# Row 8 of the first batch's q by a transposed transfer, and two subtractions on other engines

## The chip, the cores and the metric

The kernel runs on one core of a Trainium2 chip. The metric is the device time of one execution in microseconds; the runs of the kernel before took 281.86 to 282.16 us, with a median of 281.95.

## What is computed

Linear attention with a softmax on q over its 64 columns and a softmax on k over its 576 rows, and then a two-layer network with a leaky ReLU between the layers:

```python
q_s = np.exp(q - np.max(q, axis=-1, keepdims=True))
q_s = q_s / (np.sum(q_s, axis=-1, keepdims=True) + 1e-09)
k_s = np.exp(k - np.max(k, axis=2, keepdims=True))
k_s = k_s / (np.sum(k_s, axis=2, keepdims=True) + 1e-09)
kv = np.einsum('bhsd,bhse->bhde', k_s, v)
attn = np.einsum('bhsd,bhde->bhse', q_s, kv)      # q, k, v: 8 batches, 8 heads, 576 rows, 64
x = attn.transpose(0, 2, 1, 3).reshape(4608, 512)
h = x @ w_in                                       # 512 x 2048
out = np.maximum(0.01 * h, h) @ w_out              # 2048 x 512
```

## The kernel before

The 4608 rows of `x` are worked through in nine tiles of 512 (t = 0 to 8), one batch of attention being 576 rows. A tile is 64 matmuls of `layer1` (L550) and 64 of `layer2` (L571), both on TensorE (PE in the profile), with the leaky ReLU on ScalarE (ACT, L559) between them. The attention of a later batch is done in between: its steps are hung up by hand with `at(t, u, ...)` and run after step u of tile t, so that the order on every engine is fixed by the text of the kernel. Each engine works through its own instructions in that order, and waits at an instruction whose inputs are not there.

A batch's q, k and v are loaded by SyncE (SP), which issues all loads, all transposed transfers and all stores one after the other; `raw` tiles hold them as 128 partitions x 4 head pairs x 9 rows x 64. A partition holds nine rows, so the transposed q has row blocks R = 0 to 8. `H0` and `H1` are the head pairs 0, 1 and 2, 3 of the tile; `R7` is rows 0 to 6, `RE` rows 7 and 8, `R3` row 8.

For k: `k_tree` (L153, VectorE, DVE) takes the maximum over nine rows in four steps, `k_allmax` the maximum over partitions, `k_sub` (L186) subtracts it, `k_exp` (L194, ScalarE) writes `ke`. For q: `q_max` (L229), `q_sub` (L291), `q_exp` (L299), `q_sum` (L308) and `q_norm` (L315). `v_cast` (L204 on ScalarE, L206 on GpSimd, POOL) makes bf16 of v. `kv` (L328) multiplies k by v on TensorE, `kd_make` (L348, L349) divides by k's sums, and `cross` (L464) multiplies the transposed q by it. q is transposed in one of two ways: on TensorE against the identity with a copy out of PSUM (`q_turn_first` L268 with `q_keep_first` L281 and L282; `q_transpose` L432 with `q_keep` L447), or by a DMA of SyncE (`q_turn` L538, `turn_next` L544).

Tile t = 1 needs row 8 of batch 0 and rows 0 to 6 of batch 1: `attend_next` (L525) computes them at step (0, 46), in tile 0's second layer, from batch 0's transposed row 8 in `qT` and from batch 1's `X1` (heads by transposed transfer) and `qT` (heads by TensorE). The steps of batch 1 that the change touches stand at (0, 20) to (0, 45). `more_loads` and `next_loads` are the two groups of loads that SyncE issues then. Batch 2 follows in `plan2`, its matmuls against transposed q in tile 1 (`qX` and the rest of `X1`, at step (1, 27)); the loads of batch 3 are issued at (1, 2). PSUM holds six 2 KB banks in `psB_pool` and two in `psO_pool`.

The hooks and loads around the change, as they stand before it:

```python
    def more_loads():
        ...
        load(v, 1, "v_raw", [(H0, ALLR), (H1, ALLR)], t)
        st[2]["k"] = load(k, 2, "k_raw", [(H0, ALLR)])

    def next_loads():
        turn_next(slice(0, 7 * 2 * D), slice(0, 7))
        load(q, 1, "q_raw", [(ALLH, RE)], st[1]["q"])
        load(k, 2, "k_raw", [(H1, ALLR)], st[2]["k"])
```

Of the kernel before, what the change touches and what calls it, by code (L numbers as in the profile page):

```python
# [9 lines left out]
BF16 = mybir.dt.bfloat16  # L10
# [10 lines left out]
R = 9  # L21
# [4 lines left out]
def kernel(  # L26
# [9 lines left out]
    nc = tc.nc  # L36
# [10 lines left out]
    P = 128  # L47
# [27 lines left out]
    def load(src, b, name, cuts, t=None):  # L75
        t = raw(name) if t is None else t
        flat = src[b].rearrange("h s d -> (h s d)").rearrange(
            "(hl p r d) -> p hl r d", hl=HL, p=P, r=R
        )
        for hs, rs in cuts:  # L80
            nc.sync.dma_start(
                out=t[:, hs, rs].rearrange("p h r d -> p h (r d)"),
                in_=flat[:, hs, rs].rearrange("p h r d -> p h (r d)"),
            )
        return t

    ALLH, ALLR = slice(0, HL), slice(0, R)
# [95 lines left out]
    def k_sub(eng, b, hs):  # L183
        ks = st[b]["k"][:, hs]
        n = hs.stop - hs.start
        eng.tensor_tensor(  # L186
            out=ks,
            in0=ks,
            in1=st[b]["kall"][:, hs].unsqueeze(2).to_broadcast([P, n, R, D]),
            op=ALU.subtract,  # L190
        )

    def k_exp(b, hs):
        nc.scalar.activation(  # L194
            out=st[b]["ke"][:, :, hs].rearrange("p r h d -> p h r d"),
            in_=st[b]["k"][:, hs],
            func=AF.Exp,
        )
# [27 lines left out]
    def q_max(b, rs, hs=ALLH):  # L226
        n, m = rs.stop - rs.start, hs.stop - hs.start
        st[b]["qmax", rs.start, hs.start] = o = small_pool.tile([P, HL, n], FP32, name="qmax")[:, 0:m]
        nc.vector.tensor_reduce(out=o, in_=st[b]["q"][:, hs, rs], axis=AX.X, op=ALU.max)  # L229
# [58 lines left out]
    def q_sub(eng, b, rs, hs=ALLH):  # L288
        n, m = rs.stop - rs.start, hs.stop - hs.start
        qs = st[b]["q"][:, hs, rs]  # L290
        eng.tensor_tensor(  # L291
            out=qs,
            in0=qs,
            in1=st[b]["qmax", rs.start, hs.start].unsqueeze(3).to_broadcast([P, m, n, D]),
            op=ALU.subtract,
        )
# [154 lines left out]
    def cross(b, gg, outs, rows):  # L451
        for hp in range(2):
            for hh in range(2):
                half = slice(hp * D, (hp + 1) * D)
                ls = slice(hh * L, (hh + 1) * L)
                if b == 1 and rows.start == R7.stop:
                    rhs = st[b]["X1"][:, R7.stop :].rearrange("c (r g) l -> c g r l", g=2)[:, gg, :, ls]
                elif b == 1 and gg == 0:
                    rhs = st[b]["X1"][:, rows, ls]
                elif "qX" in st[b]:  # L460
                    rhs = st[b]["qX"].rearrange("c (r g) (h l) -> c g h r l", g=2, h=2)[:, gg, hh, rows]
                else:
                    rhs = st[b]["qT"][:, 2 * hh + gg, rows]
                nc.tensor.matmul(  # L464
                    outs[hp][hh * D : (hh + 1) * D].rearrange("p (r l) -> p r l", l=L),
                    lhsT=kd0[half, gg, hh, hp] if b == 0 else kd2[b % 2][half, gg, hh],
                    rhs=rhs[half],
                    start=True,
                    stop=True,
                )  # L470
# [72 lines left out]
    def turn_next(cols, blocks):  # L543
        nc.sync.dma_start_transpose(  # L544
            out=st[1]["X1"][:, blocks], in_=st[1]["qe"].rearrange("p r h d -> p (r h d)")[:, cols]
        )
# [35 lines left out]
    def at(t, u, *fns):  # L582
        while t > 0 and u >= 32:
            t, u = t + 1, u - 32
        hooks.setdefault((t, u), []).extend(fns)
# [87 lines left out]
    def more_loads():  # L673
        st[1]["v"] = t = raw("v_raw")
        nc.scalar.copy(out=t[0:1, 0, 0, 0:1], in_=identf[0:1, 0:1])
        load(v, 1, "v_raw", [(H0, ALLR), (H1, ALLR)], t)
        st[2]["k"] = load(k, 2, "k_raw", [(H0, ALLR)])

    def next_loads():
        turn_next(slice(0, 7 * 2 * D), slice(0, 7))  # L680
        load(q, 1, "q_raw", [(ALLH, RE)], st[1]["q"])
        load(k, 2, "k_raw", [(H1, ALLR)], st[2]["k"])
        st[2]["q"] = load(q, 2, "q_raw", [(ALLH, ALLR)])
        st[2]["v"] = load(v, 2, "v_raw", [(ALLH, ALLR)])
# [1 line left out]

    at(0, 20, lambda: k_begin(1), lambda: q_begin(1), lambda: k_tree(1, H0), lambda: k_tree(1, H1))
    at(0, 20, lambda: q_max(1, R7, H0), lambda: q_sub(nc.gpsimd, 1, R7, H0), lambda: k_allmax(1))
    at(0, 20, lambda: k_sub(nc.vector, 1, H1), lambda: k_sub(nc.gpsimd, 1, slice(0, 1)))
    at(0, 20, lambda: k_sub(nc.vector, 1, slice(1, 2)))  # L690
    at(0, 20, lambda: q_max(1, R7, H1), lambda: q_sub(nc.gpsimd, 1, R7, H1))
    at(0, 27, more_loads)
    at(0, 31, lambda: q_exp(1, R7, H0), lambda: q_sum(1, R7, H0), lambda: q_norm(1, R7, H0))
    at(0, 31, lambda: k_exp(1, H1), lambda: k_exp(1, H0), lambda: v_cast(nc.scalar, 1, 0))
    at(0, 32, lambda: q_exp(1, R7, H1), lambda: q_sum(1, R7, H1), lambda: q_norm(1, R7, H1))
    at(0, 32, next_loads)
    at(0, 32, lambda: v_cast(nc.scalar, 1, 1))
    at(0, 44, lambda: kv(1), lambda: kd_make(1))
    at(0, 45, lambda: q_turn_first(1, 1, R7), lambda: q_keep_first((nc.scalar, nc.vector), 1, 1, R7))
    at(0, 45, lambda: q_transpose(0, 8, 1), lambda: q_keep(nc.scalar, 0, 8, 1))  # L700
    at(0, 45, lambda: k_begin(2), lambda: q_begin(2), lambda: k_tree(2, H0, slice(0, 1)))
    at(0, 46, attend_next)
    at(1, 0, lambda: q_max(1, RE), lambda: q_sub(nc.gpsimd, 1, RE))
    at(1, 5, lambda: q_exp(1, RE))
# [3 lines left out]

    def plan2():
        b = 2  # L710
        at(1, 0, lambda: k_tree(b, H0, slice(1, 4)), lambda: k_tree(b, H1))
        at(1, 3, lambda: q_max(b, XR[0]), lambda: q_sub(nc.gpsimd, b, XR[0]))
        at(1, 3, lambda: k_allmax(b), lambda: k_sub(nc.vector, b, H0), lambda: k_sub(nc.vector, b, H1))
        at(1, 6, lambda: q_max(b, XR[1]), lambda: q_sub(nc.gpsimd, b, XR[1]))
        at(1, 11, lambda: q_exp(b, XR[0]), lambda: q_sum(b, XR[0]), lambda: q_norm(b, XR[0]))
        at(1, 13, lambda: v_cast(nc.gpsimd, b, 0), lambda: v_cast(nc.gpsimd, b, 1))
        at(1, 14, lambda: q_sum(1, RE), lambda: q_norm(1, RE))
        at(1, 15, lambda: k_exp(b, ALLH), lambda: q_turn(b, XR[0]))
        at(1, 15, lambda: turn_next(slice(7 * HL * D, R * HL * D), slice(7, 11)))
        at(1, 16, lambda: q_exp(b, XR[1]), lambda: q_sum(b, XR[1]), lambda: q_norm(b, XR[1]))  # L720
        at(1, 17, lambda: q_turn(b, XR[1]))
        at(1, 17, lambda: load_all(4))
        at(1, 23, lambda: kv(b))
        at(1, 24, lambda: kd_make(b))
        at(1, 27, lambda: attend_all(b, (XR[0],)), lambda: attend_all(1, (RE,)))
# [180 lines left out]
```

## Time and profile before

| what | value |
|---|---|
| median of the runs | 281.95 us |
| the profiled execution | 281.87 us, its span 280.1 us |
| TensorE busy | 273.5 us |
| VectorE / ScalarE / GpSimd busy | 162.0 / 160.0 / 50.1 us |
| read from HBM / written | 36.70 / 9.44 MB |

The span runs from the first to the last instruction of the program; the 1.8 us between it and the execution's time lie around it. A row of the timeline has the start, the duration, the engine, the line, the operation, out<-in and the shape; `x2` means that two equal instructions that follow each other are shown as one row, and a bracket at the end gives the idle time ahead of it and what ended it. A row of the transfers has what is written and read, the queue, the kind, the count, the size and the median time from issue to landing. The stretch of the edit on ScalarE reads:

```profile
34.79 1.16 ACT L194 ACTIVATE ke<-k_raw 128x1152 bf16<-128x1152 f32 x1 [0.85 <-DVE k_raw L186]
36.72 1.16 ACT L194 ACTIVATE ke<-k_raw 128x1152 bf16<-128x1152 f32 x1 [0.77 <-DVE k_raw L186]
37.79 1.14 ACT L204 CAST vb<-v_raw 128x1152 bf16<-128x1152 f32 x1
39.43 0.95 ACT L299 ACTIVATE qe<-q_raw 128x896 bf16<-128x896 f32 x1 [0.51 <-POOL q_raw L291]
40.29 1.14 ACT L204 CAST vb<-v_raw 128x1152 bf16<-128x1152 f32 x1
44.38 0.53 ACT L281 COPY qT<-psum_q 128x448 bf16<-128x448 bf16 x1 [2.95 <-PE psum_q L268]
44.80 0.38 ACT L447 COPY qT<-psum_qt 128x256 bf16<-128x256 bf16 x1
```

Twice there ScalarE waits for a subtraction by VectorE (L186), and once for one by GpSimd (L291).

### The profile page before, as it was taken

The page shows a single profiled execution, that of the slowest core. Times are in us where ns is not written, and L with a number is a line of the kernel's source. Part 1 is how long each engine was busy: PE and PEld are TensorE (multiplying, and loading weights), DVE is VectorE, ACT ScalarE, POOL GpSimd, SP SyncE. Part 2 cuts the span into 40 slices and gives each one's busy share as a digit, 9 for nine tenths or more (in the row PEclk, how much of TensorE's full clock was granted, in tenths as well). Part 3 has the DMA queues.
Part 4 walks back from the last instruction along what each step waited for, and adds up shares of the span by engine and source line. Part 5 has one row for each costly group of instructions (what it writes and reads, how often), then busy time and mean ns, then how long its engine had stood idle before and what let it go on. Part 6 is the DMA issues. An engine that isn't in the chain of part 4 may idle for free.

```text
span 280.1 us, 4898 instructions
## 1 busy us (share of the span) xinstructions
PE 273.5 (98%) x1963; PEld 133.4 (48%) x1963; DVE 162.0 (58%) x229; ACT 160.0 (57%) x284; POOL 50.1 (18%) x54
## 2 busy tenths in 40 slices
PE   8799999999999999999999999999999999999994
PEld 3378645444444454445444444444444444444443
DVE  2986898999999959957794588543700000000021
ACT  4977574783498277754676448744844364146400
POOL 2947530257203004000500060000000000000000
PEclk9999999999999999999999999999999999999999
DMA  7999999899692498099309930333033300330033
GB/s 245 333 209 322 248 297 328 311 325 271 214 392 81 92 363 291 1 269 396 81 0 302 361 79 2 84 77 75 1 87 75 73 4 0 75 75 2 0 75 75
DMA packets 38678, 46.15 MB, mean 165 GB/s; under 512 B 17536, under 2 KB 21888, under 8 KB 38656
## 3 DMA queue, kind: packets, MB, share of 16 engines
q1 hardware_dynamic: 35136, 41.53, 47.1%
q0 software_dynamic: 3360, 4.20, 8.6%
q8 instruction: 15, 0.25, 0.3%
q10 hardware_dynamic: 160, 0.13, 0.1%
q14 instruction: 7, 0.06, 0.1%
HBM read 36.70 MB, written 9.44 MB: 165 GB/s over the span
## 4 chain that ended last, share of the span: by engine, by line
PE 94%; DVE 2%; DMA 2%; ACT 0%; issue 0%; SPq 0%
PE pout L571 45%; PE ph L550 45%; DMA k_raw<-in_k_dram 2%; PE po L464 2%; DVE t L153 1%; PE pokv L328 1%; PE pkv L328 1%; PE pkv L406 0%; DVE k_raw L397 0%; PE psum_qt L432 0%; PE psum_q L268 0%; ACT ke L194 0%; DVE kmax L153 0%; DVE kd L421 0%; PE pokv L464 0%
## 5 line engine op out<-in xcount | busy, mean ns | idle before, releaser
L571 PE MATMUL pout<-w_out_sb,gj 128*128 128x512 bf16 (+2 forms) x592 | 127.7, 373 | 0.0
L550 PE MATMUL ph<-xT,w_in_sb 128*128 128x512 bf16 (+1 forms) x640 | 126.6, 358 | 0.0
L559 ACT ACTIVATE gj<-ph 128x512 bf16<-128x512 f32 x144 | 81.9, 602 | 25.6 <-PE ph L550 25.0
L550 PEld LDWEIGHTS <-w_in_sb 128*128 128x128 bf16 x640 | 62.3, 98 | 62.1 <-DMA w_in_sb<-in_moe_w_in_dram 0.2
L571 PEld LDWEIGHTS <-gj 128*128 128x128 bf16 x592 | 56.5, 98 | 65.3 <-issue 0.2
L565 ACT COPY out_sb<-pout 128x512 f32<-128x512 f32 (+1 forms) x29 | 16.8, 580 | 67.3 <-PE pout L571 43.3
L565 DVE COPY out_sb<-pout 128x512 f32<-128x512 f32 (+1 forms) x8 | 4.8, 636 | 70.8 <-PE pout L571 70.8
L206 POOL CAST vb<-v_raw 128x1152 bf16<-128x1152 f32 x13 | 22.9, 1785 | 81.1 <-DMA v_raw<-in_v_dram 79.4
L308 DVE TENSOR_REDUCE qsum<-qe 128x36 f32<-128x2304 bf16 (+5 forms) x13 | 20.0, 1542 | 10.3 <-ACT qe L299 10.2
L194 ACT ACTIVATE ke<-k_raw 128x1152 bf16<-128x1152 f32 (+2 forms) x12 | 17.8, 1483 | 10.0 <-DVE k_raw L186 9.9
L315 DVE TENSOR_TENSOR qe<-qe,qrec 128x2304 bf16<-128x2304 bf16 (+5 forms) x13 | 21.9, 1685 | 0.4
L229 DVE TENSOR_REDUCE qmax<-q_raw 128x36 f32<-128x2304 f32 (+5 forms) x13 | 20.0, 1539 | 0.6 <-DMA q_raw<-in_q_dram 0.6
L299 ACT ACTIVATE qe<-q_raw 128x2304 bf16<-128x2304 f32 (+5 forms) x13 | 17.1, 1317 | 4.1 <-POOL q_raw L291 3.2
L186 DVE TENSOR_TENSOR k_raw<-k_raw,kall 128x1152 f32<-128x1152 f32 (+2 forms) x10 | 19.2, 1943 | 0.4
L153 DVE TENSOR_TENSOR t<-t 128x256 f32<-128x256 f32 (+2 forms) x22 | 15.6, 710 | 0.7
L487 ACT CAST xT<-po 128x448 bf16<-128x448 f32 (+3 forms) x34 | 14.4, 518 | 1.1 <-PE po L464 1.1
L291 POOL TENSOR_TENSOR q_raw<-q_raw,qmax 128x512 f32<-128x512 f32 (+3 forms) x7 | 10.8, 1547 | 22.1 <-DVE qmax L229 21.0
L291 DVE TENSOR_TENSOR q_raw<-q_raw,qmax 128x2304 f32<-128x2304 f32 (+1 forms) x6 | 13.2, 2202 | 0.3
L348 DVE RECIPROCAL krec<-pokv 128x2 f32<-128x2 f32 x8 | 1.3, 165 | 20.1 <-PE pokv L464 20.1
L153 DVE TENSOR_TENSOR t<-k_raw 128x512 f32<-128x512 f32 (+1 forms) x11 | 12.3, 1115 | 0.7 <-DMA k_raw<-in_k_dram 0.5
L360 PE MATMUL pout<-zero 128*128 128x512 f32 (+3 forms) x18 | 8.4, 587 | 1.0 <-POOL zero L100 1.0
L328 PEld LDWEIGHTS <-ke 64*64 64x64 bf16 x504 | 5.9, 107 | 3.4 <-issue 2.5
(70 smaller groups left out, 107.0 us busy)
## 6 DMA issues: line engine op xcount, KB each, us to landing
out_dram<-out_sb SPq DMA_DIRECT2D x70, 128.0 KB, 2.5
q_raw<-in_q_dram SPq DMA_DIRECT2D x6, 1152.0 KB, 8.7
v_raw<-in_v_dram SPq DMA_DIRECT2D x6, 1152.0 KB, 11.4
k_raw<-in_k_dram SPq DMA_DIRECT2D x5, 1152.0 KB, 6.5
k_raw<-in_k_dram SPq DMA_DIRECT2D x6, 576.0 KB, 6.2
v_raw<-in_v_dram SPq DMA_DIRECT2D x4, 576.0 KB, 7.6
w_in_sb<-in_moe_w_in_dram POOLq DMA_DIRECT2D x8, 256.0 KB, 6.9
w_out_sb<-in_moe_w_out_dram POOLq DMA_DIRECT2D x6, 256.0 KB, 9.2
```

Of the source, the lines that this page charges most:

```text
L153: nc.vector.tensor_tensor(out=o, in0=i0, in1=i1, op=ALU.max)
L186: eng.tensor_tensor(out=ks, in0=ks, in1=st[b]["kall"][:, hs].unsqueeze(2).to_broadcast([P, n, R, D]), op=ALU.subtract,)
L194: nc.scalar.activation(out=st[b]["ke"][:, :, hs].rearrange("p r h d -> p h r d"), in_=st[b]["k"][:, hs], func=AF.Exp,)
L206: eng.tensor_copy(out=o, in_=i)
L229: nc.vector.tensor_reduce(out=o, in_=st[b]["q"][:, hs, rs], axis=AX.X, op=ALU.max)
L291: eng.tensor_tensor(out=qs, in0=qs, in1=st[b]["qmax", rs.start, hs.start].unsqueeze(3).to_broadcast([P, m, n, D]), op=ALU.subtract,)
L308: nc.vector.reduce_sum(out=qsum, in_=q_cols(b, rs, hs), axis=AX.X)
L315: nc.vector.tensor_tensor(out=qes, in0=qes, in1=st[b]["qrec", rs.start, hs.start].unsqueeze(3).to_broadcast([P, n, m, D]), op=ALU.mult,)
L550: nc.tensor.matmul(ph, lhsT=w_in_sb[:, cb, j * P : (j + 1) * P], rhs=xT[:, cb, c0 : c0 + n], start=(cb == 0 and first), stop=(cb == NB - 1 ...
L559: nc.scalar.activation(out=o, in_=ph, func=AF.Prelu, alpha=LEAKY_SLOPE)
L565: copy(out=out_sb, in_=pout)
L571: nc.tensor.matmul(pout, lhsT=g_sb[j // 2][:, j % 2, tsub * P : (tsub + 1) * P], rhs=w_out_sb[:, j, os], start=(j == 0), stop=(j == NF - 1),)
```

## The change

Row 8 of batch 0's normalised q is transposed by a transfer of 128 x 256 bf16 (64 KB) into a new tile `X8`, issued by SyncE right behind batch 1's transposed transfer; the two matmuls of L432 and the copy L447 that did it go. The first load of batch 2's k moves from the end of `more_loads` to behind both transfers. GpSimd subtracts the maximum from both k heads of `H0` of batch 1 (it did head 0, VectorE head 1), and VectorE does q's second subtraction, which GpSimd did. On ScalarE the exponential of q's second half goes ahead of k's `H0` and of the first cast of v. The first step of batch 2's maximum over k goes from (0, 45) to (1, 0), where the others stand.

```diff
@@ cross
-                if b == 1 and rows.start == R7.stop:
+                if b == 0 and rows.start == R3.start:
+                    rhs = st[b]["X8"][:, gg : gg + 1, ls]
+                elif b == 1 and rows.start == R7.stop:
@@ more_loads, next_loads
-        st[2]["k"] = load(k, 2, "k_raw", [(H0, ALLR)])
 
     def next_loads():
         turn_next(slice(0, 7 * 2 * D), slice(0, 7))
+        st[0]["X8"] = const_pool.tile([P, 2, P], BF16, name="X8")
+        nc.sync.dma_start_transpose(out=st[0]["X8"], in_=st[0]["qe"][:, R - 1].rearrange("p h d -> p (h d)"))
+        st[2]["k"] = load(k, 2, "k_raw", [(H0, ALLR)])
         load(q, 1, "q_raw", [(ALLH, RE)], st[1]["q"])
@@ the hooks of tile 0
-    at(0, 20, lambda: k_sub(nc.vector, 1, H1), lambda: k_sub(nc.gpsimd, 1, slice(0, 1)))
-    at(0, 20, lambda: k_sub(nc.vector, 1, slice(1, 2)))
-    at(0, 20, lambda: q_max(1, R7, H1), lambda: q_sub(nc.gpsimd, 1, R7, H1))
+    at(0, 20, lambda: k_sub(nc.vector, 1, H1), lambda: k_sub(nc.gpsimd, 1, H0))
+    at(0, 20, lambda: q_max(1, R7, H1), lambda: q_sub(nc.vector, 1, R7, H1))
     at(0, 27, more_loads)
     at(0, 31, lambda: q_exp(1, R7, H0), lambda: q_sum(1, R7, H0), lambda: q_norm(1, R7, H0))
-    at(0, 31, lambda: k_exp(1, H1), lambda: k_exp(1, H0), lambda: v_cast(nc.scalar, 1, 0))
-    at(0, 32, lambda: q_exp(1, R7, H1), lambda: q_sum(1, R7, H1), lambda: q_norm(1, R7, H1))
+    at(0, 31, lambda: k_exp(1, H1), lambda: q_exp(1, R7, H1), lambda: k_exp(1, H0))
+    at(0, 31, lambda: v_cast(nc.scalar, 1, 0))
+    at(0, 32, lambda: q_sum(1, R7, H1), lambda: q_norm(1, R7, H1))
     at(0, 32, next_loads)
     at(0, 32, lambda: v_cast(nc.scalar, 1, 1))
     at(0, 44, lambda: kv(1), lambda: kd_make(1))
     at(0, 45, lambda: q_turn_first(1, 1, R7), lambda: q_keep_first((nc.scalar, nc.vector), 1, 1, R7))
-    at(0, 45, lambda: q_transpose(0, 8, 1), lambda: q_keep(nc.scalar, 0, 8, 1))
-    at(0, 45, lambda: k_begin(2), lambda: q_begin(2), lambda: k_tree(2, H0, slice(0, 1)))
     at(0, 46, attend_next)
@@ plan2
-        at(1, 0, lambda: k_tree(b, H0, slice(1, 4)), lambda: k_tree(b, H1))
+        at(1, 0, lambda: k_begin(b), lambda: q_begin(b), lambda: k_tree(b, H0), lambda: k_tree(b, H1))
```

## The prediction

> **What bounds the kernel now.** I read the busy shares first, then the chain of waits in order of time, then the timeline of each engine around the edit.
>
> ```profile
> span 280.1 us, 4898 instructions
> PE 273.5 (98%) x1963; PEld 133.4 (48%) x1963; DVE 162.0 (58%) x229; ACT 160.0 (57%) x284; POOL 50.1 (18%) x54
> PEclk9999999999999999999999999999999999999999
> PE 94%; DVE 2%; DMA 2%; ACT 0%; issue 0%; SPq 0%
> ```
>
> TensorE is busy for 98% of the span at its full granted clock, and 94% of the chain that ended last is TensorE. The other engines count only where TensorE has to wait for them. The chain where the edit falls:
>
> ```profile
> 42.24 0.73 PE pkv L328 x72
> 42.98 0.97 PE pout L571 x4
> 43.95 0.39 PE psum_q L268 x7
> 44.34 0.11 PE psum_qt L432 x2
> 44.45 0.86 PE pout L571 x4
> 45.31 0.56 PE po L464 x16
> 45.88 0.97 PE pout L571 x4
> ```
>
> Every piece begins where the one before it ends: from 14.33 us to 276.35 the chain holds TensorE and, at 20.52, 0.04 us of issue, and nothing else. So a microsecond saved on another engine is worth nothing, TensorE work taken out is worth itself, and a new wait of TensorE costs itself. The sum runs against the profiled execution (281.87 us, 280.1 of it span); the median of the three runs, 281.95, is 0.08 above it, so I add the difference to the median.
>
> **Part 1: two transposes and their copy go.** The `psum_qt` piece at 44.34 is 0.11 us long: two matmuls, 0.055 apart like the seven of L268 before them (0.39 / 7). Gain 0.11 us. ScalarE's copy out of PSUM (L447, one of 378 ns at 44.80) goes too; ScalarE was off the chain, worth 0. Matmuls that read row 8 now wait for the transfer X8 instead. The second group also waits for VectorE's copy L282 (44.94 to 45.33), which doesn't move; in the timeline these matmuls start at 45.49, in future 45.38, so 0.05 us of cover is left there.
>
> **Part 2: the subtractions change engines.** Rows of VectorE and GpSimd:
>
> ```profile
> 34.68 1.96 DVE L186 TENSOR_TENSOR k_raw<-k_raw,kall 128x576 f32<-128x576 f32 x1
> 33.45 2.58 POOL L186 TENSOR_TENSOR k_raw<-k_raw,kall 128x576 f32<-128x576 f32 x1 [0.49 <-DVE kall L178]
> 37.71 1.69 POOL L291 TENSOR_TENSOR q_raw<-q_raw,qmax 128x896 f32<-128x896 f32 x1 [1.69 <-DVE qmax L229]
> ```
>
> VectorE's 1152 elements take 1.36 (33.40 to 34.76). GpSimd's 576 take 2.58 beside it, and VectorE's own 576 take 1.96, more than the larger one. The times fit turns: GpSimd starts when VectorE ends at 34.76 and needs 1.27, to 36.02; VectorE then needs 0.61, to 36.64. Alone, GpSimd takes 1.08 for 512, 1.68 for 896 and 2.76 for 1536 elements, so 1152 is about 2.1. New order: VectorE subtracts heads 2, 3 until 34.76 and reduces q's maximum (1.07) until 35.75; GpSimd runs 34.76 to 36.9; VectorE's subtraction of q's 896 waits until 36.9, then takes about 0.95 (0.61 x 896 / 576), to 37.85. Before, this maximum ended at 37.63, so the sum and the multiply behind it begin 0.2 later; but the multiply took 1.41 behind GpSimd's 1.69 row and 1.09 without it, so it ends at about 40.3, as before (40.35). The transposed transfer of batch 1 is issued then, as now.
>
> ScalarE: exp of heads 2, 3 ends at 35.95; exp of q 37.9 to 38.85 (0.95); exp of heads 0, 1 (1.16) to 39.95; two casts (1.14 each, 0.1 overlapped) to 42.0. Before, the last cast ended at 41.42. TensorE reads its half after the first 36 matmuls of the 42.24 piece, at about 42.5, so 0.5 of cover is left. Cost 0; without the cover it would be what exceeds 0.5.
>
> **Part 3: the new transfer.** SyncE's queue and its landings:
>
> ```profile
> 40.41 1.34 SPq L544 DMA_TRANSPOSE X<-qe  x1
> X<-qe SPq DMA_TRANSPOSE x1, 4.1
> qX<-qe SPq DMA_TRANSPOSE x1, 2.5
> ```
>
> The first transposed transfer holds SyncE for 1.34 and lands 4.1 after its start, behind batch 2's first k (issued 30.99, landed 12.7 later, at 43.7). The last row is that at 70.48, with no load ahead of it: 2.5. X8 is issued when the first leaves SyncE, at about 41.7, and lands between 44.2 (2.5) and 45.85 (4.1). TensorE wants it at 45.2 less 0.11, at 45.13. The k load that made the first one slow is now behind it, so I take 2.5: 0.9 of cover, cost 0; by the upper end 0.7 of stall. The Trainium skill ("DMA: Bandwidth & Descriptors", Rules for kernel authors) speaks against a transfer this small: up to 64 KB it is mostly overhead. The rows agree on the issue (1.19 for four blocks, 1.34 for seven), and that is priced next. [...]
>
> **Part 4: everything queued behind it.** On SyncE, k's first half moves from 30.99 to about 43.0, and rest of q 1, k's second half, q 2 and v 2 are issued some 1.6 later than 41.80 to 43.53.
>
> ```profile
> k_raw<-in_k_dram SPq DMA_DIRECT2D x1, 576.0 KB, 12.7
> v_raw<-in_v_dram SPq DMA_DIRECT2D x1, 1152.0 KB, 11.1
> 47.75 7.38 SPq L568 DMA_DIRECT2D out_dram<-out_sb  x8
> 55.23 0.54 SPq L81 DMA_DIRECT2D k_raw<-in_k_dram  x1
> v_raw<-in_v_dram SPq DMA_DIRECT2D x1, 1152.0 KB, 11.9
> X<-qe SPq DMA_TRANSPOSE x1, 2.9
> ```
>
> v 2 lands at 43.53 + 11.1 = 54.65; the eighth store is issued then (54.67), batch 3's loads behind it from 55.23, v 3 lands at 56.46 + 11.9 = 68.3, and the transposes of batch 2 (issued 65.98, landing 69.9) and of batch 1's rest (67.41, landing 70.3) follow in the same queue. TensorE reads them at 71.79 and 72.14. Call the slip of this train s. Its lower bound: 0.59 MB more in front, at the 400 GB/s of the 46 to 54 us stretch 1.4, less up to 0.6 that one late engine of the sixteen may regain: 0.8. Its upper bound: the memory has been idle, and a 1152 KB load issued at 71.79 after transposes took 6.4 to land, so k's half lands at 43.0 + 6.4 - 1.4 = 48.0, the rest of q some 0.7 to 1.0 behind (0.7 in the landings 44.5 and 45.2), k's second half 1.4 to 1.7 behind that, by 50.7 against 48.0 before: 2.7. I take 1.5, nearer to the bytes. Cover: X would land at 71.8 while TensorE, 0.11 early, needs it at 72.03; the point from which it stalls is s = 1.6. Cost at 1.5: 0. All readers in between have more: the row maximum of q 1's rest at 49.2 against a landing by 49.0, k's second half at 51.7 against 50.7, q 2 at 54 against 53.5.
>
> VectorE: the first maximum step of batch 2's k (0.69 at 45.25) moves behind the four stores' copies. Before, it held the first cast to xT at 45.85; that now runs at 45.6. So the train after 49.4 is later by 0.69 - 0.24 = 0.45, and by up to 0.7 if GpSimd's subtraction at 50.2 comes between its steps. kd of batch 2 ended at 71.23, 0.5 before TensorE read it; see the third rival. ScalarE then reaches exp of batch 3's k just as it is ready (79.16); behind it, six activations run without a gap, while TensorE has six PSUM buffers, so 0.7 there stalls nothing.
>
> Sum: -0.11 + 0 + 0 + 0. 281.95 - 0.11 = **281.84, say 281.85 us**, which no measurement of this kernel tells from no change: runs spread by 0.1%, and I count 0.2% (0.56 us) as the least that can be told.
>
> **Rivals.** First, on the other side: the load train slips past its cover. For it: it is one queue in order, two transposes deep, ending 1.8 before a reader. Against: bytes alone make 1.4. Stall = s - 1.6: at 2.2, 281.84 + 0.6 = 282.4; at 2.7, 282.9. Chance 0.32, with 0.20 of it at s above 2.3, where the cold start stays whole.
>
> Second: X8 lands late, as the 4.1 row. Then TensorE stands from 45.13 to 45.85: 282.55. Against it, the k load is gone from in front. Chance 0.08, 0.06 of it past 282.5.
>
> Third: the order of GpSimd and VectorE at 69 us. Before, GpSimd's cast of v 3 (start 68.47) made VectorE's multiply at 68.54 take 1.88 for 768 elements; 0.94 is the reduction of as many. VectorE will come at 69.2. If v 3 lands after that, VectorE goes first and kd is ready at 71.0. If it lands at 68.7 to 69.1, GpSimd holds it until 70.3, the multiply ends at 71.2, kd at 72.05: a stall of up to 0.4, 282.2, and more only with another wait beside it (0.02 of its chance). The Trainium skill ("SBUF — State Buffer", Who interferes with whom) says that such a pair is locked for a whole instruction and that issue order decides who blocks; the rows at 34.68 agree. Chance 0.08.
>
> Fourth: the change gives nothing, because the matmuls at 45.38 meet L282's copy late: 281.95. Chance 0.04. A gain over 0.56 has no row behind it, TensorE having no other idle time; 0.05 for what I can't see. The forecast keeps 0.43.
>
> **The numbers.** Slower by over 0.2% (past 282.51): 0.20 of the first rival, 0.06 of the second, 0.02 of the third, 0.28. Faster: 0.05. Same: 0.43 + 0.12 + 0.02 + 0.06 + 0.04 = 0.67. Range 281.65 to 282.8: from the full gain less the spread of the runs to s = 2.55, which leaves out about 0.15.
>
> **What would show it.** Right: the chain has no psum_qt, TensorE's pieces at 45 and 72 us abut, X8 lands before 45.1, GpSimd's 1152 elements end near 36.9, v 3 lands at 69.8. Wrong: weight loads of L466 idle on a transfer at 45 or at 72, a kd that ends after 71.6, or ScalarE's last v cast after 42.5.

## The result, and the profile after

The changed kernel takes 283.26 us (median of 10 runs, 282.13 to 283.66) against 282.0 us for the kernel before on the same chip (10 runs, 281.73 to 282.26): 1.0041 times as long, 95% interval 1.0032 to 1.0049. That is slower by 1.26 us, beyond the 0.2% that can be told from no change; one of the ten runs, at 282.13, lies among those of the kernel before, the others from 282.86 on. The profiled execution took 283.44 us, 1.57 more than the one before.

The first lines of its page: the span, TensorE's busy time, and the shares of the chain that ended last.

```profile
span 281.6 us, 4894 instructions
PE 274.1 (97%) x1961; PEld 133.4 (47%) x1961; DVE 162.1 (58%) x229; ACT 159.7 (57%) x283; POOL 51.1 (18%) x53
PE 82%; DMA 9%; DVE 2%; POOL 2%; SPq 1%; issue 1%; ACT 1%; DVEq 0%; ACTq 0%
```

TensorE's share of the chain fell from 94% to 82%, and the transfers' rose from 2% to 9%. That says not that 12% were lost, but that the chain can now be followed back through other engines to the first load, because somewhere TensorE waited. The place is in the chain in order of time (start, length, what):

```profile
36.52 2.42 DVE q_raw L291
...
39.82 1.15 ACT ke L194
40.96 1.05 ACT vb L204
42.02 0.70 SPq L546
42.76 4.11 DMA X<-qe
...
46.92 0.64 PE po L466 x16
47.55 0.97 PE pout L573 x4
48.52 13.81 PE ph L552 x64
```

A transfer of 4.11 us that starts at 42.76 stands where TensorE stood before, and from 46.92 on the chain is TensorE alone again, as it was from 14.33 on in the kernel before. The transfer is `X8`: `X` would be issued a step earlier. Behind it the `pout` piece that began at 45.88 begins at 47.55, 1.67 later. TensorE's own timeline (start, busy time, line, shape, and in brackets the idle time before and what ended it):

```profile
42.22 0.48 PE L328 MATMUL pkv<-vb,ke 64*64 64x65 bf16 x36
43.11 0.48 PE L328 MATMUL pkv<-vb,ke 64*64 64x65 bf16 x36 [0.41 <-ACT vb L204]
...
44.78 1.03 PE L573 MATMUL pout<-w_out_sb,gj 128*128 128x512 bf16 x4
46.92 0.44 PE L466 MATMUL po<-X,kd 64*64 64x64 bf16 x12 [1.11 <-DMA X<-qe]
```

There are two waits: 0.41 us for ScalarE's last cast of v, and 1.11 us for `X8`. (The 0.26 between 1.52 of waits and the 1.78 of later start, the 0.11 saved being added, lies in pieces around them which the view does not count as idle.) The first wait adds nothing by itself, since `X8` lands at a moment that TensorE does not set: without it, TensorE would have stood that much longer at 46.9. `X8` alone decides.

Its neighbours are shown by the transfers between its issue and its landing (queue, kind, packets, megabytes and share of the sixteen engines; then issues with the median time to landing):

```profile
q1 hardware_dynamic: 1344, 0.67, 65.7%
q8 instruction: 1, 0.02, 1.9%
...
X<-qe SPq DMA_TRANSPOSE x1, 4.1
```

`X8` takes 4.1 us to land although batch 2's k load is behind it. A single packet of another kind lies beside it: an instruction fetch, 16,384 bytes, in the packet records from 44.52 to 45.77. The chain and the list of waits do not point at it; of the views only the queue list has it. That it matters had to be shown.

### The profile page after: what moved, and what is told of

Read it like the earlier page. It is cut to its first block, busy times and chain, and to the rows that moved or that the text cites. A ratio compares the mean times of both kernels' runs of the same rounds, so it can differ in the third digit from the quotient of the medians.

```text
span 281.6 us, 4894 instructions
## 1 busy us (share of the span) xinstructions
PE 274.1 (97%) x1961; PEld 133.4 (47%) x1961; DVE 162.1 (58%) x229; ACT 159.7 (57%) x283; POOL 51.1 (18%) x53
## 4 chain that ended last, share of the span: by engine, by line
PE 82%; DMA 9%; DVE 2%; POOL 2%; SPq 1%; issue 1%; ACT 1%; DVEq 0%; ACTq 0%
PE pout L573 40%; PE ph L552 39%; DMA q_raw<-in_q_dram 3%; DMA w_in_sb<-in_moe_w_in_dram 2%; DMA k_raw<-in_k_dram 2%; DMA X<-qe 1%; PE po L466 1%; SPq L81 1%; PE pokv L328 1%; DVE q_raw L291 1%; DVE qmax L229 1%; POOL w_in_sb L126 1%; PE pkv L328 1%; ACT ke L194 0%; POOL vb L206 0%
## 5 line engine op out<-in xcount | busy, mean ns | idle before, releaser
L206 POOL CAST vb<-v_raw 128x1152 bf16<-128x1152 f32 x13 | 24.0, 1875 | 78.1 <-DMA v_raw<-in_v_dram 66.6
L315 DVE TENSOR_TENSOR qe<-qe,qrec 128x2304 bf16<-128x2304 bf16 (+5 forms) x13 | 20.7, 1589 | 0.4
L186 DVE TENSOR_TENSOR k_raw<-k_raw,kall 128x1152 f32<-128x1152 f32 (+1 forms) x9 | 17.3, 1941 | 0.4
L291 DVE TENSOR_TENSOR q_raw<-q_raw,qmax 128x2304 f32<-128x2304 f32 (+2 forms) x7 | 16.5, 2353 | 0.3
L153 DVE TENSOR_TENSOR t<-t 128x256 f32<-128x256 f32 (+2 forms) x22 | 14.7, 669 | 0.7
L291 POOL TENSOR_TENSOR q_raw<-q_raw,qmax 128x512 f32<-128x512 f32 (+3 forms) x6 | 9.4, 1568 | 24.4 <-DVE qmax L229 23.4
L360 PE MATMUL pout<-zero 128*128 128x512 f32 (+3 forms) x18 | 9.0, 619 | 1.0 <-POOL zero L100 1.0
L328 PEld LDWEIGHTS <-ke 64*64 64x64 bf16 x504 | 5.9, 107 | 3.9 <-issue 2.6
```

Of the source, the lines that this page charges most:

```text
L153: nc.vector.tensor_tensor(out=o, in0=i0, in1=i1, op=ALU.max)
L186: eng.tensor_tensor(out=ks, in0=ks, in1=st[b]["kall"][:, hs].unsqueeze(2).to_broadcast([P, n, R, D]), op=ALU.subtract,)
L206: eng.tensor_copy(out=o, in_=i)
L291: eng.tensor_tensor(out=qs, in0=qs, in1=st[b]["qmax", rs.start, hs.start].unsqueeze(3).to_broadcast([P, m, n, D]), op=ALU.subtract,)
L315: nc.vector.tensor_tensor(out=qes, in0=qes, in1=st[b]["qrec", rs.start, hs.start].unsqueeze(3).to_broadcast([P, n, m, D]), op=ALU.mult,)
```

## The experiments

Ratios are to the kernel before on the same chip, with 95% intervals; ranges are lowest to highest run (5 to 12 runs each).

| kernel | median us (range) | ratio |
|---|---|---|
| changed kernel | 283.26 (282.13 to 283.66) | 1.0041 [1.0032, 1.0049] |
| engines swapped only | 282.13 (281.75 to 282.36) | 1.0002 [0.9993, 1.0010] |
| k load moved only | 282.10 (281.80 to 282.48) | 0.9999 [0.9991, 1.0008] |
| `X8` behind `X` only | 283.04 (281.92 to 283.77; one at 580.77 left out) | 1.0030 [1.0018, 1.0042] |
| changed, `X8` early | 282.04 (281.89 to 282.40) | 1.0000 [0.9992, 1.0009] |
| changed, engines not swapped | 282.82 (281.86 to 284.34) | 1.0027 [1.0011, 1.0044] |
| changed, `X8` early, not swapped | 281.85 (281.55 to 283.85) | 0.9992 [0.9984, 1.0001] |
| `X8` early only | 281.72 (281.51 to 282.84) | 0.9997 [0.9987, 1.0007] |
| changed, 49 wakes | 299.07 (298.82 to 299.67) | 1.0600 [1.0587, 1.0614] |
| changed, 112 small matmuls | 283.11 (282.10 to 284.70) | 1.0042 [1.0025, 1.0060] |
| before, 112 small matmuls | 282.07 (281.73 to 282.86) | 1.0006 [0.9997, 1.0014] |
| changed, 88 small matmuls | 282.77 (281.99 to 283.77) | 1.0029 [1.0018, 1.0040] |
| k load moved only, 88 | 281.87 (281.52 to 282.50) | 0.9997 [0.9988, 1.0005] |
| `X8` behind `X` only, 88 | 281.83 (281.60 to 282.15) | 0.9997 [0.9988, 1.0006] |
| before, 88 | 282.16 (281.97 to 282.91) | 1.0010 [1.0001, 1.0019] |
| changed, 72 | 283.04 (282.88 to 283.78) | 1.0039 [1.0025, 1.0053] |

### Each part alone

**The swap of engines**, on the kernel before:

```diff
-    at(0, 20, lambda: k_sub(nc.vector, 1, H1), lambda: k_sub(nc.gpsimd, 1, slice(0, 1)))
-    at(0, 20, lambda: k_sub(nc.vector, 1, slice(1, 2)))
-    at(0, 20, lambda: q_max(1, R7, H1), lambda: q_sub(nc.gpsimd, 1, R7, H1))
+    at(0, 20, lambda: k_sub(nc.vector, 1, H1), lambda: k_sub(nc.gpsimd, 1, H0))
+    at(0, 20, lambda: q_max(1, R7, H1), lambda: q_sub(nc.vector, 1, R7, H1))
...
-    at(0, 31, lambda: k_exp(1, H1), lambda: k_exp(1, H0), lambda: v_cast(nc.scalar, 1, 0))
-    at(0, 32, lambda: q_exp(1, R7, H1), lambda: q_sum(1, R7, H1), lambda: q_norm(1, R7, H1))
+    at(0, 31, lambda: k_exp(1, H1), lambda: q_exp(1, R7, H1), lambda: k_exp(1, H0))
+    at(0, 31, lambda: v_cast(nc.scalar, 1, 0))
+    at(0, 32, lambda: q_sum(1, R7, H1), lambda: q_norm(1, R7, H1))
```

> The kernel before with the change of engines and of ScalarE's order alone (GpSimd subtracts k heads 0 and 1, VectorE q's second half); transposes and loads as before. Theory A (the loss is TensorE's wait for X8): no wait at 45 us, time as before, ratio 1.000 to 1.0005. Theory B (GpSimd's 1152 elements make ScalarE's last cast of v late): GpSimd ends about 2.5 us after VectorE's 1152, the last cast ends 1.0 to 1.6 us later than before, TensorE stands 0.1 to 0.6 us inside L328, ratio 1.0005 to 1.002.

Measured 1.0002: no cost that can be told. In its profile ScalarE's last cast of v held TensorE between the two groups of L328 (1.04 us for both from 42.18, against 0.80 in the profile before), and the run still came out at 282.13. The part alone is not the cause.

**The move of batch 2's k load**, with the step of the maximum:

```diff
@@ more_loads, next_loads
-        st[2]["k"] = load(k, 2, "k_raw", [(H0, ALLR)])
...
         turn_next(slice(0, 7 * 2 * D), slice(0, 7))
+        st[2]["k"] = load(k, 2, "k_raw", [(H0, ALLR)])
...
-    at(0, 45, lambda: k_begin(2), lambda: q_begin(2), lambda: k_tree(2, H0, slice(0, 1)))
...
-        at(1, 0, lambda: k_tree(b, H0, slice(1, 4)), lambda: k_tree(b, H1))
+        at(1, 0, lambda: k_begin(b), lambda: q_begin(b), lambda: k_tree(b, H0), lambda: k_tree(b, H1))
```

> The kernel before with batch 2's first load of k behind batch 1's transposed transfer (and the first maximum step over it at (1, 0)), nothing else. Theory A and B: no cost, ratio 1.000. Theory C (the load train slips past its cover): batch 3's v lands 1.5 to 2.5 us later than before (68.3), the transposed q of batch 2 lands after TensorE wants it at 71.7, a stall of 0 to 0.7 us there, ratio 1.000 to 1.0025.

Measured 0.9999. The load of v of batch 3 landed at 70.79 us, 2.47 later than in the profile before, and `qX` behind it at 72.20: the train does slip by nearly the prediction's upper bound, yet nothing could be told. (In the profiled run a late load of weights held TensorE until 22.50, and the `pout` piece of 45.88 began at 46.35, 0.47 later than before, so that run may have had more cover than its fellows.)

**`X8` behind `X`**, with the k load left ahead of both:

```diff
+                if b == 0 and rows.start == R3.start:
+                    rhs = st[b]["X8"][:, gg : gg + 1, ls]
...
         turn_next(slice(0, 7 * 2 * D), slice(0, 7))
+        st[0]["X8"] = const_pool.tile([P, 2, P], BF16, name="X8")
+        nc.sync.dma_start_transpose(out=st[0]["X8"], in_=st[0]["qe"][:, R - 1].rearrange("p h d -> p (h d)"))
...
-    at(0, 45, lambda: q_transpose(0, 8, 1), lambda: q_keep(nc.scalar, 0, 8, 1))
```

> The kernel before with row 8 of batch 0 by the transfer behind batch 1's, the load of k left ahead of both, engines as before. Theory A: X8 is issued at 41.8 and lands at 45.2 to 46.9, TensorE stands 0.1 to 1.7 us at 45.1, ratio 1.000 to 1.006. Theory B: no wait inside L328; ratio 0.9996 unless X8 is late.

Measured 1.0030, most of the loss. The runs fell in two groups, three at 281.92 to 282.17 and eight at 283.00 to 283.77: something is met or missed. The profiled execution is the one at 580.77 and is not read; the kernel was profiled a second time.

> The kernel of e3_x8_only again, for its profile. Theory A1: a 16 KB instruction fetch overlaps X8's completion and it lands 3.5 to 4.5 us after its issue at about 41.8; TensorE waits 0.3 to 1.7 us at 45.1 us. Theory A2: it lands as late with no fetch beside it.

It took 283.21. TensorE's timeline, and the transfers from the issue of `X8` to its landing:

```profile
46.70 0.44 PE L466 MATMUL po<-X,kd 64*64 64x64 bf16 x12 [1.46 <-DMA X<-qe]
```

```profile
q8 instruction: 1, 0.02, 1.8%
...
X<-qe SPq DMA_TRANSPOSE x1, 4.4
```

The wait is there without the swap and without the move of the k load, and so is the fetch, at 44.34 here.

### The same transfer, issued early

```diff
         load(v, 1, "v_raw", [(H0, ALLR), (H1, ALLR)], t)
+        st[0]["X8"] = const_pool.tile([P, 2, P], BF16, name="X8")
+        nc.sync.dma_start_transpose(out=st[0]["X8"], in_=st[0]["qe"][:, R - 1].rearrange("p h d -> p (h d)"))
...
         turn_next(slice(0, 7 * 2 * D), slice(0, 7))
-        st[0]["X8"] = ...
-        nc.sync.dma_start_transpose(...)
```

On the changed kernel, with everything else as changed:

> The changed kernel with X8 issued right behind batch 1's loads of v (at about 31 us), all else as changed. Theory A: the wait at 45 us goes, the time falls by about 1.2 us from the changed kernel's, to a ratio of 1.001 to 1.002 of the kernel before. Theory B: the stall of about 0.57 us inside L328 stays. Theory C: with the wait at 45 us gone, one at 72 us shows, 0 to 0.9 us.

Measured 1.0000, below the 1.001 to 1.002 that was expected. `X8` is issued at 31.11 and lands at 42.41, and the pieces abut both at 45 and at 72 us:

```profile
44.39 1.03 PE L573 MATMUL pout<-w_out_sb,gj 128*128 128x512 bf16 x4
45.35 0.47 PE L466 MATMUL po<-X,kd 64*64 64x64 bf16 x12
```

So with `X8` early nothing of the loss can be told, and the swap and the k move together cost nothing that can be told in this order of the queue (`X8` no longer stands between `X` and the k load). Three more take the parts apart further. The changed kernel with the swap undone and `X8` where the change put it:

> The changed kernel with the subtractions and ScalarE's order as before (GpSimd k head 0 and q's second half, VectorE k head 1); X8 and the load of k as changed. Theory A: no wait inside L328; X8 still lands 2.7 to 4.2 us after an issue at 41.8, TensorE waits 0.3 to 1.7 us at 45.1, ratio 1.002 to 1.0055. Theory B (the swap makes the loss): ratio 0.9996 to 1.001.

Measured 1.0027, again in two groups (four runs at 281.86 to 281.93, the others from 282.62): the loss does not need the swap. With the swap undone and `X8` early, and with early `X8` as the only edit to the kernel before:

> The changed kernel with X8 issued behind batch 1's loads of v, and the subtractions and ScalarE's order as before; the load of k behind batch 1's transposed transfer as changed. Theory A: no wait, ratio 0.9993 to 1.0003, like e4. Theory B (the swap costs once X8 is early): 0.0005 to 0.002 below e4's 1.0000.

> The kernel before with X8 issued right behind batch 1's loads of v and ahead of batch 2's first k, and the two transposes and their copy gone; nothing else. Theory A: X8 lands by 43 us, no wait, TensorE's two transposes (0.11 us) are saved: ratio 0.9992 to 1.0002. If the queue pays for it (batch 2's k behind it, then batch 1's transposed transfer later than 45.1): ratio 1.001 to 1.004.

Measured 0.9992 and 0.9997, both intervals holding 1. No version that beats the kernel before was found: the 0.11 us of the two transposes, 0.04%, is under what these runs can tell. (The profiled run of the first of the two was its longest by far, with waits for weights of 0.50 and 0.94 us that end at 37.12 and 39.94, and is not read.)

### Why it lands late: moving the fetch

In each of the four profiles in which `X8`, issued behind `X`, was late (changed kernel, `X8` alone, swap undone, 112 small matmuls), a fetch began between its issue and its landing; in the five in which it was not late, none did. The packet records (not a view of the page) give times in us; 4-byte packets are the completion writes, 32 for this transfer:

```
                            issue  last data  30th 4-byte  last 4-byte  landed  fetch
changed                     42.76    44.41       44.81        45.76     46.88   44.52 to 45.77
changed, 112 small matmuls  42.56    44.18       44.60        46.03     47.07   44.59 to 46.03
changed, 49 wakes           58.86    60.50       60.89        60.91     61.21   none
changed, 88 small matmuls   42.21    43.83       44.22        44.25     44.55   none
```

The data are over 1.62 to 1.65 us after the issue in all four. What comes late is the last two of the small writes, and these sit at the end of the fetch. (So they do with `X8` alone, at 45.62 with a fetch to 45.62; with the swap undone they come at 46.70, 0.46 behind the end of the fetch. The landing then follows by 1.0 to 1.1 in the first two rows and by 0.3 in the others, which no view explains.) The Trainium skill ("DMA: Bandwidth & Descriptors", Queues, rings and completion order) says that a completion write lands only after every earlier write of its DMA engine, across the queues of that engine. The trace of the changed kernel agrees, 30 writes out by 44.81 and the last at 45.76 with the fetch's end at 45.77; but the records do not name the engine of a packet, so that the late writes and the fetch share one is inferred.

A fetch came at about every 250 of TensorE's instructions, weight loads counted (in the changed kernel 15 packets for 3922 of them); the queue's name does not say whose instructions these are, and that they are TensorE's rests on this count and on what follows. Instructions added to the start, where TensorE waits for data anyway, should therefore move the fetches. In the first version of this the wakes (matmuls on zeros at the start) were cut into many:

```diff
-    wake(TT, TT, TT, 256)
+    wake(TT, *[32] * 32, *[16] * 16)
```

> The changed kernel with the start-up matmuls on zeros cut finer (same columns in 49 instead of 4 pieces, 45 program matmuls more), so that the 16 KB fetches of TensorE's instructions fall some 180 instructions earlier in the program. Theory A1 (X8's completion waits behind the fetch that starts at 44.5 us on one DMA engine): no fetch between 43 and 46.5 us, X8 lands 2.5 to 2.9 us after its issue instead of 4.1, TensorE waits 0 to 0.5 us instead of 1.2, ratio 1.000 to 1.002. Theory A2 (a transfer behind another transposed one takes 4 us by itself): it lands 4 us after its issue, ratio 1.0035 to 1.005 as the changed kernel.

The time is of no use: the small fp32 wakes took about 0.215 us an instruction however few columns they had, and the start became 17 us longer. The profile is: no fetch lay beside `X8`, which landed 2.35 us after its issue. But that run's memory traffic around it was another. Small bf16 matmuls on the identity, `quads(n)` for n of 64 x 64 by 64, replaced two wakes instead:

```diff
-    wake(256)
+    quads(28)
+    wake(P)
...
-    wake(384)
+    quads(84)
```

> The changed kernel with 112 small matmuls on the identity at 9 and 11 us in place of start-up matmuls on zeros of about the same time, so that some 220 more TensorE instructions stand ahead of the stretch and its fetches fall elsewhere (at about 33 us, and not before TensorE has passed 45 us). Theory A1 (X8's completion waits behind the 16 KB fetch): no fetch between 43.5 us and X8's landing, which comes 2.3 to 2.8 us after its issue instead of 4.1; TensorE waits 0 to 0.4 us; time 1 us or more below the changed kernel's, to 1.000 to 1.0015 of the kernel before plus what the start costs (the control shows it). Theory A2: it lands 4 us after its issue, ratio 1.0035 to 1.005.

> Control: the kernel before with the same 112 small matmuls at the start. Both theories: the start costs 0 to 0.4 us, ratio 1.000 to 1.0015; batch 1's transposed transfer lands about as before.

These are the changed kernel and, as a control, the kernel before. The first failed: the fetch came at 44.59 again, since some 220 instructions more are nearly one whole interval. `X8` was late once more, and the ratio, 1.0042, as that of the changed kernel. The fetch, `X8`'s landing and TensorE's wait:

```profile
q8 instruction: 1, 0.02, 2.0%
...
X<-qe SPq DMA_TRANSPOSE x1, 4.5
```

```profile
47.12 0.44 PE L476 MATMUL po<-X,kd 64*64 64x64 bf16 x12 [1.52 <-DMA X<-qe]
```

So small matmuls alone, without moving the fetch away, do not make `X8` land sooner. The second kernel, the control, says that the added matmuls alone cost nothing that can be told, 1.0006. With 88 of them (`quads(28)`, `quads(60)` and a `wake(P)` behind each):

> The changed kernel, with 88 small identity matmuls in place of two wake matmuls of the start-up (where TensorE waits for data anyway), so that some 175 TensorE instructions more precede batch 0's end. Nothing else differs. The instruction fetches of 16 KB in the packet records came at about every 250 of TensorE's instructions (weight loads counted): at 719 in the changed kernel (44.52 us) and at 949, that is 727 without the added ones, in the version with 112. By these counts the fetches should here fall near 38 us and near 48 us, and none between X8's issue (42.8) and 47. Fetch theory: X8 lands 2.3 to 2.8 us after its issue, by 45.6, TensorE waits 0 to 0.4 for it, and the ratio to the kernel before is 0.9995 to 1.002. Rival (a second transposed transfer close behind the first lands after 4 to 4.5 us whatever lies beside it): X8 lands at 46.8 or later, the wait is 1.2 to 1.7, ratio 1.003 to 1.005. The control (the kernel before with 112 such matmuls) stood at 1.0006.

The transfers from the issue of `X8` to its landing, and TensorE's timeline:

```profile
q1 hardware_dynamic: 1177, 0.29, 53.1%
...
X<-qe SPq DMA_TRANSPOSE x1, 2.3
```

```profile
44.23 1.03 PE L583 MATMUL pout<-w_out_sb,gj 128*128 128x512 bf16 x4
45.19 0.47 PE L476 MATMUL po<-X,kd 64*64 64x64 bf16 x12
...
73.18 0.52 PE L476 MATMUL po<-qX,kd 64*64 64x384 bf16 x8 [1.34 <-DMA qX<-qe]
```

No fetch, 2.3 us, and the matmuls at 45 us start as soon as the piece before them ends. Yet the ratio is 1.0029, not the 1.0 to 1.002 of the expectation: a wait of 1.34 us has come up at 71.8 us, for batch 2's transposed `qX`. The theory stood for `X8` and fell short for the total. Four more kernels and a second profile of this one went at that. First the version with `X8` alone, and the same 88 matmuls added:

> The kernel before with X8 alone behind X (batch 2's first k stays ahead of both; this stood at 1.003 without the small matmuls, X8 landing 4.44 us after its issue) and with the 88 small start-up matmuls, which take the fetch away from 44 us. Fetch theory: X8 lands 2.3 to 3 us after its issue, TensorE waits 0 to 0.3 for it, no stall at 72 us (v of batch 3 lands by 69.6, the k load not being moved), ratio 0.9990 to 1.0007. Rival (X8 is late because it is the second transposed transfer, or because of the k load ahead): 4 us or more, wait 1 to 1.6, ratio 1.002 to 1.004.

This is the cleanest pair of the study: the kernel that loses by `X8` alone, with the same 88 matmuls. Its ratio goes from 1.0030 [1.0018, 1.0042] to 0.9997 [0.9988, 1.0006], and its runs from two groups to one (281.60 to 282.15). The transfers from the issue of `X8` to its landing, and TensorE:

```profile
q1 hardware_dynamic: 1227, 0.32, 91.8%
q0 software_dynamic: 46, 0.04, 9.0%
...
X<-qe SPq DMA_TRANSPOSE x1, 2.8
```

```profile
44.27 1.03 PE L583 MATMUL pout<-w_out_sb,gj 128*128 128x512 bf16 x4
45.22 0.47 PE L476 MATMUL po<-X,kd 64*64 64x64 bf16 x12
```

The k load is ahead of it here and it lands in 2.8 all the same. The control, the kernel before with these 88 matmuls:

> Control: the kernel before with the 88 small start-up matmuls and nothing else. Ratio 0.9990 to 1.0010; a value above it would be the price of the matmuls, or of a fetch at 70.5 us beside qX, which lands 1.8 before TensorE reads it in the kernel before.

The control stands at 1.0010, so the matmuls (or where they put the other fetches) cost at most a little, and the gain of the pair is not theirs.

### The second wait

The version with the k load moved alone, and the 88 matmuls added:

> The kernel before with batch 2's first k load moved alone (as in the version that stood at 0.9999) and with the 88 small start-up matmuls, so that TensorE's instruction fetch comes at about 70.5 us instead of about 66. If the second stall (1.3 us in front of qX at 71.5 in the profile of the changed kernel with these matmuls) comes of a load train that ends late together with a fetch beside qX, TensorE waits 0.5 to 1.5 here at 71 to 73 us, qX lands 5 us or more after its issue, and the ratio is 1.0015 to 1.004. Rival (the train alone, whatever lies beside it): then the version without the small matmuls would have lost as much, which it did not; ratio 0.9995 to 1.0005 here would mean that the second stall needs X8's place in the queue as well.

Measured 0.9997: the k move alone, with the fetch beside `qX` (at 69.55), does not bring the second wait. My expectation of 1.0015 or more fell. v of batch 3 landed at 67.83 here, at 68.15 with `X8` alone and at 66.39 in the control, but at 70.20 in the changed kernel with the same matmuls, which has both. Against the control, the two parts delay the train by 1.4 and 1.8 and together by 3.8. These are single profiles: v's landing spreads by 1.9 among those that leave the train as it was (66.39 to 68.32). The changed kernel with 88 matmuls was profiled again:

> The changed kernel with the 88 small start-up matmuls, profiled once more. X8 lands 2.3 to 2.8 us after its issue and TensorE does not wait for it. At 71 to 73 us TensorE waits for qX: 0.3 to 1.5, by how long v of batch 3 and the fetch at 70.5 hold it up; the other runs of this kernel, 0.3 to 1.4 below the profiled one, had less of it.

`X8` landed in 2.34 us, and TensorE waited at 72 us as before:

```profile
73.43 0.52 PE L476 MATMUL po<-qX,kd 64*64 64x384 bf16 x8 [1.47 <-DMA qX<-qe]
```

In both profiles a fetch lies beside `qX` again, at 70.50 and 71.08. Whether the late train suffices without it was the question of the last run, with 72 matmuls (`quads(44)` and a `wake(256)` in place of the second pair):

> The changed kernel with 72 small start-up matmuls instead of 88. By the counts so far every fetch comes about 32 TensorE instructions later: near 41 us (over before X8's data) and, in place of 70.5, near 73 us, behind qX's landing. X8 lands 2.3 to 2.8 us after its issue, as with 88. If the second stall needs the fetch beside qX, v of batch 3 lands at 70.0 to 70.9, qX 1.4 behind it (as in the changed kernel and with the k move alone, where no fetch lay there), TensorE waits 0 to 0.3 for it and the ratio is 0.999 to 1.001. If the late load train is enough by itself, qX lands at 72.5 or later, TensorE waits 0.7 or more and the ratio is 1.002 or more. Should a fetch still lie between 69 and 72 us, the run decides nothing.

Measured 1.0039, but a fetch still lay there, at 71.41, so by its own terms it does not decide. Its waits of TensorE from 40 to 80 us (in total, times, longest):

```profile
PE po L476 <- DMA qX<-qe: 1.4, 1, 1.4
PE po L476 <- DMA X<-qe: 0.3, 1, 0.3
```

What can be said: in these three, v landed at 70.20 to 70.69 and `qX` 2.9 to 3.1 behind it, with a fetch; in the changed kernel and with the k move alone v landed later still, at 70.87 and 70.79, and `qX` 1.4 behind it, without one. That points at the fetch for some 1.5 us, and at the late train for bringing `qX` that close to its reader. As an estimate: with 1.4 behind v, `qX` would have landed at 71.60 to 72.09 in these three, and TensorE came for it 0.2 to 0.3 later, so the train alone would not have made it wait for `qX`. It was not shown by a run of this kernel without the fetch. The nearest is the changed kernel with `X8` early, its v of batch 3 issued at 58.52 (59.67 with 88 matmuls, 56.46 in the profile before) and no fetch beside `qX`, which landed at 71.28, 0.64 before TensorE read it. The cause of the second wait stays open to that extent.

## Why the prediction was wrong

The forecast was 281.85 us, no change that can be told; the kernel is slower, at 283.26, outside the range.

**The step that failed is the sum's third term.** Part 3 said: "The k load that made the first one slow is now behind it, so I take 2.5: 0.9 of cover, cost 0." The k load is indeed what slows `X`: with it ahead, `X` lands 3.6 to 4.1 us after its issue in the five profiles that have no fetch before the landing (the kernel before, the swap alone, both controls, `X8` alone with 88); with it behind, after 2.7. And 2.5 is about right for a transfer left in peace: 2.3 to 2.8 in the five profiles without a fetch beside it. What I missed is that a second thing makes such a transfer land late: TensorE's own instruction fetch, which meets `X8` at 44.3 to 44.8 and for which the sum has no term. In the profile before it is there too, at 44.72, and does no harm, `X` having landed at 44.55. I read the row of 4.1 for its cause and let the cause remove it; the queue list of the page, which has the fetches, I did not lay beside the new transfer. In place of the cost of 0, TensorE's next piece began 1.67 us later.

The issue time failed with it. `X8` was issued at 42.76, not 41.7. Of this 1.06, 0.73 is VectorE's late start of the row in this execution (its first subtraction ended at 35.49, not 34.76, after a load that landed 0.73 later), and most of the rest is part 2's: the multiply ahead of `X` ended at 41.32, 0.97 later than before. One profile had been taken for the time of `X`'s issue, 40.41; of the others (leaving out the version with 49 wakes and the run of 580.77) all but one have it later, up to 42.09. The later issue does not simply add to the stall. In the quiet landings with the k load behind, the last small write came 2.04 to 2.05 after the issue; a transfer issued at 41.7 would have been written by 43.75, before the fetch began at 44.52. That is an estimate, and so is what it suggests for the two groups of runs: in the version with 112 matmuls 30 writes were out by 44.60 and the fetch began at 44.59, so a small difference in time decides. No run of the faster group was profiled.

The upper end of that part, 4.1 and 0.7 of stall, had the duration right by chance: the row of 4.1 is a transfer behind a k load, this one a transfer beside a fetch. My second rival, `X8` late as the row of 4.1, is the case that came true in its size; it had a chance of 0.08, because what it named against itself, the k load gone from in front, was not what made this transfer late.

**Part 1 held.** TensorE goes from L268 straight to `pout` at 44.78; the two matmuls of L432 at 44.18 and the copy are gone. Its 0.11 us can't be told in any of the early versions (0.9992, 0.9997).

**Part 2 was mis-sized, but its own wait added nothing.** GpSimd's row, VectorE's subtraction behind it and ScalarE's last casts:

```profile
34.18 3.80 POOL L186 TENSOR_TENSOR k_raw<-k_raw,kall 128x1152 f32<-128x1152 f32 x1 [0.48 <-DVE kall L178]
```

```profile
36.52 2.40 DVE L291 TENSOR_TENSOR q_raw<-q_raw,qmax 128x896 f32<-128x896 f32 x1
```

```profile
40.87 2.19 ACT L204 CAST vb<-v_raw 128x1152 bf16<-128x1152 f32 x2
```

The turns were read rightly: GpSimd's row runs from 34.18 to 37.98, and VectorE's subtraction of q, begun at 36.52, ends at 38.93, 0.95 behind it. From the end of VectorE's own subtraction (35.49) GpSimd took 2.49, not 2.1: the forecast took its pace from rows in which it ran alone, while the row beside VectorE, 1.27 for 576 elements, gives 2.54 for twice as many. With the 0.73 of the late start, the last cast of v ended at 43.06, where 42.0 was forecast and 42.5 was the limit: the 0.41 of TensorE's wait at 43.11. The swap alone stood at 1.0002, so nothing of this can be told in the time.

**Part 4 was mis-sized and hid.** v of batch 3 landed at 70.87, which makes s 2.55, not the 1.5 taken, and near the upper bound of 2.7 (that the memory had been idle, which that bound supposed, was not tested). The stall point was misread by 0.1: `X` at 70.3 and a reader at 72.03 give 1.7, not 1.6. By it an s of 2.55 should have cost 0.85. It cost nothing in the changed kernel because TensorE, by then 1.67 behind, came to `qX` at 73.47 (landed 72.25) and to `X` at 73.82 (landed 72.75). With the k move alone nothing could be told either (0.9999): in its profile TensorE met `qX` and `X` as they landed, at 72.26 and 72.74, 0.5 and 0.6 later than before, in a run in which TensorE was 0.47 late already; and the profile before, with v at 68.32, was a late base to count s from, since v landed at 67.82 with the swap alone and at 66.39 in the control, neither of which touches the train. So there is up to 1.9 more of cover in other executions. But with `X8` freed of its fetch a wait came up where the first rival had put it: v at 70.20, `qX` at 73.14, a wait of 1.34. By the rival's own sum, s less 1.6, an s of 1.88 would have cost 0.3; a fetch lay beside `qX`, and how much of the wait is the train's stays open. Losses at 45 and at 72 us do not simply add: in the changed kernel the first gave the second its cover. So taking away the first one brought back at most part of the time (1.0041 to 1.0029, intervals that overlap).

**The third rival** did not show: TensorE has no idle time on `kd` at 72 us in any profile. **The fourth** can't be told apart from the forecast's own gain.

## What to carry to other kernels

A transfer that TensorE reads within some 4.5 us of its issue needs the slow landing in the sum, not the quiet one: lay it beside every queue of the profile, the instruction queue too, whose fetches came here at about every 250 of TensorE's instructions and moved when instructions were added ahead of them. Take the time of its issue from more than one execution. Where the source is ready early, issue the transfer early; here that took away all of the loss that can be told, at no cost that can be told. After a stall has been cured, look for the next one behind it before the gain is booked.

## What the hardware showed that was not expected

A transposed transfer of 64 KB, issued behind another one, landed 2.34 to 2.75 us after its issue with no instruction fetch beside it, and 3.98 to 4.51 with one. Counted from the start of the fetch the late ones agree: 2.36, 2.31, 2.64 and 2.48 us (changed kernel, `X8` alone, swap undone, 112 matmuls). One packet of 16 KB, 1.25 to 1.44 us long, thus went with a landing later by more than its own length. With 72 matmuls the fetch, at 41.84, lay beside `X` instead: that landed 3.48 us after its issue, against 2.7 in the eight profiles with the k load behind it and no fetch, and `X8` behind it took 2.35.

A small matmul in fp32 showed a floor here. In the version with 49 wakes (each fp32 wake is two instructions in the trace), the row of these matmuls in the groups by shape (count, then busy us and mean ns of one, then idle time before):

```profile
L360 PE MATMUL pout<-zero 128*128 128x32 f32 x64 | 13.7, 399 | 0.0
```

That is 0.214 us each (13.7 / 64) for 32 columns; those with 16 columns took 7.0 us for 32, 0.219 each. Fewer columns saved nothing; the weight loads of these and the other wakes took 23.5 us for 108, 0.218 each, so the floor is probably theirs.
